# Batch 0's column attention and its reading of x placed among units 2 and 3, the table load placed first, and a new instruction order

## The chip, the cores and the metric

The kernel runs on one core of a Trainium2 chip. The metric is the device time of one execution in microseconds (us), lower being better. TensorE is called PE, VectorE DVE, ScalarE ACT, GpSimd POOL; SP is the engine whose queue issues most of the DMAs.

## The reference

Attention in two directions between x (8 batches, 8 heads, 512 positions, 64 wide) and a state (32 rows per head), and a feed-forward layer over the 4608 joined rows, with a rational function between its two products:

```python
a = softmax(scale * x @ state.T, over the state rows)          # row attention
xread = a @ state
a2 = softmax(scale * state @ x.T, over the 512 positions)      # column attention
sread = a2 @ x
X = concat([xread, sread], axis=2), heads joined to 512 columns # 4608 x 512
h = X @ w_in                                                   # 512 -> 2048
P = a[0] + a[1]*h + a[2]*h*h + a[3]*h*h*h
Q = 1 + |b[0]|*|h| + |b[1]|*h*h
out = (P / (Q + 1e-6)) @ w_out                                 # 2048 -> 512
```

## The kernel before, in words

**Units.** The hidden width of 2048 is cut into 8 slices of 256. Unit n is batch n // 8 with slice n % 8; units 64 to 71 are the 256 sread rows of all batches. A unit's tiles are 128x1024. Its steps, each a token of the order below: `F:n:0` and `F:n:1` (front, L818; 6 matmuls of 512 columns each) make h in PSUM; ACT makes `FC` (C, L830) and `FB` (A, L837); DVE runs `mu` (L841), `po` (L845) and `qd` (L851), which read h in PSUM; ACT `qa`, `ln`, `ex` (L857, L928, L938) make the reciprocal; DVE `g1` (gh, L862), `g2` (L868), `g3` (L874); POOL `gl` (L881). The second product is `mh:n:t` (4 matmuls with gh) and `ml:n:t` (2 matmuls with gl), for four groups t of 128 rows (L891); they add up over 8 units in four PSUM banks o0 to o3. h stays in its PSUM tile until `po`.

**Front of a batch.** xread is never formed: a unit multiplies the row attention aT with m = state times a slice of w_in. `X:i` (L715, 32 small matmuls) makes m for two batches, `XA:i` copies it out of PSUM on ACT (L733), `xs:i` stores it and `lm`, `fs`, `ft` load and split it later (a high and a low part, so that fp32r matmuls keep the precision). For batch 0 `fh` and `fo` (L747 on ACT, L751 on DVE) take it straight from PSUM.

**Weights.** They come in as 64-bit words and are turned into fp32 on the chip, in groups 0 to 15 of 1 MB (slices of w_in and w_out in turns): `lr` loads a half on SP's queue, `cp` (ACT, L300), `jr` (DVE, L313) and `jl` (DVE, L331) convert; for w_out `wh` (ACT, L346) and `wl` (POOL, L353) split it. The tiles `cv_y` and `cv_r` of `cp` and `jr` share four buffers; the result of a w_out group lies in `cv_r` until both `wl` are done. `ws` stores a converted slice, `lw` loads it again for later batches.

**Attention of batch 0.** It is made in halves by its own functions: `scores0:g` (PE, L397 in `scores`), `sc_copy0:g` (ACT, L533), `row_T0:g` (PE, L547), `row_max0`, `row_sub0`, `row_sum0` (DVE, L568 to L587), `row_exp0` (ACT), `row_norm0` (POOL, L592), `a_T0`, `a_hi0`, `a_lo0` (L596 to L614), which make aT for units 0 to 7. Its column attention is `col_max:0` (L414), `col_scale:0` (L418), `col_exp:0:j` (ACT, L444), `col_eps:0`, `col_norm:0` (L472, L476), the transposes `e2_T0:j` (L616, into o2 and o3) and copies `e2_copy0:j` (L621), then `sread:0:g` (PE, L638, reads x), `sr_copy:0` (L650), `sr_T:0`, `sr_fin:0` (L661). Nothing but units 64 to 71 needs its result. Batches 1 to 7 use `e2_T` and `e2_copy` (L481, L486) with one tile of two banks.

**PSUM.** Beside o0 to o3 there are two tiles of two banks each, tag "h" (`ps_h`), shared by h, the X tiles, scores, `e2_T` and sread.

**Order.** `ORDER` is a list of tokens, found by a search and written out by hand; the loop at the end calls one function for each token, and each engine issues its instructions in that order. So a token that waits holds back all later ones on its own engine, and no others. Cross-engine waits and the choice of a free buffer are made when the program is built. `pre` loads the activation table set; `lc`, `cb`, `cv`, `b0a` bring in the constants; `ls:a:b` loads the state of batches a to b - 1 (on ACT's queue if a is 0, else SP's); `lx` loads the next piece of x or of x transposed, in the order in which they are used.

Of the kernel before, what the change touches and what calls it, by code (L numbers as in the profile page):

```python
# [199 lines left out]
def attention_rational_ffn(  # L200
# [159 lines left out]
    def load_win(n):  # L360
# [3 lines left out]
        win_t[n] = t  # L364

    TS, AT, X = {}, {}, {}
    xseq, x_at = [], [0]  # L370

    def load_next_x():
        i = x_at[0]
        if i == len(xseq):
            return
        x_at[0] += 1
# [689 lines left out]
```

## Time and profile before

| what | value |
|---|---|
| median of 3 runs | 663.66 us (663.57 to 663.66) |
| profiled execution | 663.7 us, its span 661.9 us |
| PE busy | 642.4 us, 97% of the span |
| DVE busy | 622.2 us, 94% |
| ACT busy | 520.3 us, 79% |
| POOL busy | 310.1 us, 47% |
| DMA moved | 85.67 MB |
| mean granted clock of PE | 0.996 of full |

Busy time is the time in which an engine has an instruction running; matmuls overlap, so a busy PE need not be at its peak. The span runs from the first instruction's start to the last one's end. A row of the time line gives the start, the length, the engine, the line of the kernel, and in brackets how long the engine sat idle before and what ended that.

### The profile page before, as it was taken

The page shows a single profiled execution, that of the slowest core. Times are in us where ns is not written, and L with a number is a line of the kernel's source. Part 1 is how long each engine was busy: PE and PEld are TensorE (multiplying, and loading weights), DVE is VectorE, ACT ScalarE, POOL GpSimd, SP SyncE. Part 2 cuts the span into 40 slices and gives each one's busy share as a digit, 9 for nine tenths or more (in the row PEclk, how much of TensorE's full clock was granted, in tenths as well). Part 3 has the DMA queues.
Part 4 walks back from the last instruction along what each step waited for, and adds up shares of the span by engine and source line. Part 5 has one row for each costly group of instructions (what it writes and reads, how often), then busy time and mean ns, then how long its engine had stood idle before and what let it go on. Part 6 is the DMA issues. An engine that isn't in the chain of part 4 may idle for free.

```text
span 661.9 us, 11289 instructions
## 1 busy us (share of the span) xinstructions
PE 642.4 (97%) x4474; PEld 509.8 (77%) x4474; DVE 622.2 (94%) x585; ACT 520.3 (79%) x634; POOL 310.1 (47%) x174
## 2 busy tenths in 40 slices
PE   5689999999999999999999999999999999999997
PEld 2556677877878877878878888878788888888995
DVE  5999999899998997999999999999999999899886
ACT  5989999887968688877777887859787768784772
POOL 1254346535454434545443564445554454455550
PEclk9999999999999999999999999999999999999999
DMA  9969987144417162314213220204322010101411
GB/s 346 407 213 394 328 303 254 34 143 138 143 45 245 52 239 97 128 48 144 82 50 125 100 93 17 80 32 144 109 83 81 32 65 32 49 33 51 142 49 32
DMA packets 30679, 85.67 MB, mean 129 GB/s; under 512 B 3490, under 2 KB 3618, under 8 KB 30626
## 3 DMA queue, kind: packets, MB, share of 16 engines
q1 hardware_dynamic: 30290, 84.56, 36.4%
q8 instruction: 35, 0.57, 0.4%
q10 hardware_dynamic: 336, 0.39, 0.3%
q14 instruction: 18, 0.15, 0.1%
HBM read 57.15 MB, written 27.79 MB: 128 GB/s over the span
## 4 chain that ended last, share of the span: by engine, by line
PE 91%; ACT 4%; DVE 2%; issue 1%; POOL 1%; DMA 1%; ACTq 0%; POOLq 0%
PE h L818 29%; PE ps_x L715 3%; PE o__1521 L891 2%; PE o__2974 L891 2%; PE o__5848 L891 2%; PE o__1530 L891 2%; PE o__2242 L891 2%; PE o__4128 L891 2%; PE o__4759 L891 2%; PE o__2979 L891 2%; PE o__4143 L891 2%; PE o__2215 L891 2%; PE o__2250 L891 2%; PE o__2199 L891 2%; PE o__4167 L891 2%; PE o__3564 L891 2%
## 5 line engine op out<-in xcount | busy, mean ns | idle before, releaser
L881 POOL TENSOR_TENSOR gl<-C,L 128x1024 fp32r<-128x1024 f32 (+1 forms) x70 | 171.4, 2451 | 226.3 <-DVE C L874 155.2
L818 PE MATMUL h<-aT,m 128*128 128x512 f32 x768 | 186.9, 391 | 0.2 <-ACT xo_w L733 0.2
L818 PEld LDWEIGHTS h<-aT,m 128*128 128x128 f32 x768 | 143.4, 188 | 32.6 <-ACT xo_w L733 1.0
L830 ACT ACTIVATE C<-h,cst 128x1024 f32<-128x1024 f32 (+1 forms) x72 | 83.3, 1157 | 38.9 <-PE h L818 26.5
L764 POOL TENSOR_TENSOR m<-m_sb,m 128x512 fp32r<-128x512 f32 x56 | 81.7, 1463 | 59.8 <-ACT m L760 56.1
L862 DVE SCALAR_TENSOR_TENSOR gh<-C,cst,L 128x1024 fp32r<-128x1024 f32 (+1 forms) x72 | 93.3, 1297 | 9.9 <-ACT L L938 8.2
L837 ACT ACTIVATE A<-h,cst 128x1024 f32<-128x1024 f32 (+1 forms) x72 | 76.8, 1066 | 30.1 <-PE h L818 24.0
L851 DVE SCALAR_TENSOR_TENSOR A<-A,b0a,h 128x1024 f32<-128x1024 f32 (+1 forms) x72 | 87.2, 1213 | 4.7 <-ACT A L837 3.6
L874 DVE SCALAR_TENSOR_TENSOR C<-C,cst,A 128x1024 f32<-128x1024 f32 (+1 forms) x72 | 89.4, 1244 | 1.5
L845 DVE SCALAR_TENSOR_TENSOR C<-C,cst,h 128x1024 f32<-128x1024 f32 (+1 forms) x72 | 87.5, 1218 | 1.7
L857 ACT ACTIVATE A<-A 128x1024 f32<-128x1024 f32 (+1 forms) x72 | 72.8, 1011 | 19.8 <-DVE A L851 19.8
L868 DVE SCALAR_TENSOR_TENSOR A<-A,gh 128x1024 f32<-128x1024 f32 (+1 forms) x72 | 86.5, 1201 | 1.8
L841 DVE TENSOR_TENSOR C<-C,h 128x1024 f32<-128x1024 f32 (+1 forms) x72 | 82.9, 1152 | 1.8 <-ACT C L830 1.8
L928 ACT ACTIVATE L<-A 128x1024 f32<-128x1024 f32 (+1 forms) x72 | 73.0, 1013 | 3.0
L938 ACT ACTIVATE L<-L 128x1024 f32<-128x1024 f32 (+1 forms) x72 | 72.7, 1013 | 1.7
L715 PE MATMUL ps_x<-win_sb,st 64*32 64x256 f32 x1024 | 35.8, 393 | 3.3 <-ACT xo_w L733 1.8
L760 ACT CAST m<-m_sb 128x512 fp32r<-128x512 f32 x56 | 34.2, 613 | 4.0 <-PE h L818 3.7
L353 POOL TENSOR_TENSOR wo<-cv_r,wo 128x512 fp32r<-128x512 f32 x16 | 24.7, 1564 | 22.1 <-ACT wo L346 22.1
L715 PEld LDWEIGHTS ps_x<-win_sb,st 64*32 64x32 f32 x1024 | 17.4, 109 | 18.7 <-issue 5.9
L818 PEld LDWEIGHTS h<-sh,m 128*128 128x128 f32 x192 | 23.9, 191 | 0.6
L818 PE MATMUL h<-sh,m 128*128 128x256 f32 x192 | 24.1, 283 | 0.0
L733 ACT COPY xo<-ps_x 128x1024 f32<-128x1024 f32 (+1 forms) x24 | 20.7, 872 | 1.5 <-PE ps_x L715 1.3
(245 smaller groups left out, 1106.6 us busy)
## 6 DMA issues: line engine op xcount, KB each, us to landing
m_sb<-m_dram SPq DMA_DIRECT2D x56, 256.0 KB, 3.1
xT_sb<-in_xT_dram SPq DMA_DIRECT2D x16, 512.0 KB, 5.5
x_sb<-in_x_dram SPq DMA_DIRECT2D x16, 512.0 KB, 5.7
m_dram<-xo SPq DMA_DIRECT2D x16, 512.0 KB, 3.7
win_sb<-w_in_dram SPq DMA_DIRECT2D x16, 512.0 KB, 4.3
out_dram<-o_sb SPq DMA_DIRECT2D x32, 256.0 KB, 3.5
raw<-in_w_in_dram SPq DMA_DIRECT2D x10, 512.0 KB, 8.1
raw_w<-in_w_out_dram SPq DMA_DIRECT2D x8, 512.0 KB, 8.8
```

The source lines that it names most:

```text
L764: nc.gpsimd.tensor_tensor(m[:, 1], MF.pop(n), m[:, 0].bitcast(F32), op=ALU.subtract)
L818: nc.tensor.matmul(h[:, ci * W : (ci + 1) * W], l, r, start=(q == 0), stop=(q == len(seq) - 1),)
L830: nc.scalar.activation(e["C"], e["h"], AF.Identity, scale=cst[:, 3:4], bias=cst[:, 2:3])
L837: nc.scalar.activation(e["A"], e["h"], AF.Abs, scale=cst[:, 5:6])
L841: nc.vector.tensor_tensor(e["C"], e["C"], e["h"], op=ALU.mult)
L845: nc.vector.scalar_tensor_tensor(e["C"], e["C"], cst[:, 1:2], e["h"], op0=ALU.add, op1=ALU.mult)
L851: nc.vector.scalar_tensor_tensor(e["A"], e["A"], b0a, e["h"], op0=ALU.add, op1=ALU.mult)
L862: nc.vector.scalar_tensor_tensor(e["gh"], e["C"], cst[:, 0:1], e["L"], op0=ALU.add, op1=ALU.mult)
L868: nc.vector.scalar_tensor_tensor(e["A"], e["A"], 1.0 + 1e-6, e["gh"].bitcast(F32), op0=ALU.add, op1=ALU.mult)
L874: nc.vector.scalar_tensor_tensor(e["C"], e["C"], cst[:, 0:1], e["A"], op0=ALU.add, op1=ALU.subtract)
L881: eng.tensor_tensor(e["gl"], e["C"], e["L"], op=ALU.mult)
L891: nc.tensor.matmul(O[t], e[l][:, j * W + x : j * W + x + P], WO[u][:, j, k, :], start=(u == 0 and l == "gh" and k == 0 and j == 0), stop=( ...
```

## The change

The order list is new throughout. Up to unit 3 it differs as shown; behind that it is again a list of the same tokens with other neighbours. Batch 0's column attention, which stood ahead of units 0 and 1 and between them, now stands among units 1 to 3 (`col_max:0` ahead of `g1:1`, `sread:0` behind `g1:2`), and uses `e2_T` and `e2_copy` with a two-bank tile, as the other batches do; `e2_T0` and `e2_copy0` are gone. `pre` stands ahead of the first copy on ACT. The first state load brings one batch instead of two. Loads of x and of x transposed are tokens of their own with batch and half (`lx:b:g`, `lt:b:g`); from batch 4 on the transposed x uses the buffers of the X copies (tag "xo").

```diff
--- before.py
+++ after.py
 ORDER = [
-    "ls:0:2 lx scores0:0 sc_copy0:0 lr:0:0 cp:0:0 jr:0:0 jl:0:0 row_T0:0 pre lc cb row_max0:0 "
-    "row_sub0:0 lx cv b0a scores0:1 sc_copy0:1 lr:0:1 jr:0:1 cp:0:1 col_max:0 jl:0:1 row_T0:1 "
-    "col_scale:0 row_exp0:0 row_max0:1 row_sub0:1 row_sum0:0 ls:2:8 col_exp:0:0 col_exp:0:1 lr:1:0 "
-    "cp:1:0 X:1 row_norm0:0 lr:1:1 row_exp0:1 row_sum0:1 XA:1 X:0 jr:1 fh:0 XA:0 row_norm0:1 cp:1:1 "
-    "X:2 XA:2 fo:0 jl:1 a_T0:0 a_hi0:0 a_lo0:0 a_T0:1 X:4 a_hi0:1 a_lo0:1 lr:2:0 cp:2:0 lr:2:1 jr:2 "
-    "F:0:0 F:0:1 cp:2:1 col_eps:0 col_norm:0 XA:4 lr:3:0 jl:2 fh:1 fo:1 F:1:0 lr:4:0 cp:4:0 cp:3:0 "
-    "lr:3:1 cp:3:1 F:1:1 jr:3 jl:3 e2_T0:1 lr:4:1 FB:0 jr:4 FC:0 wh:3 wl:3:1 FB:1 qd:0 lx mu:0 lx "
-    "lr:5:0 lr:5:1 qa:0 ln:0 ex:0 qd:1 e2_T0:0 po:0 wl:3:0 e2_copy0:0 e2_copy0:1 sread:0:0 sread:0:1 "
-    "lr:6:0 lr:6:1 cp:5:0 jr:5 g1:0 mh:0:3 ws:0 xs:1 g2:0 cp:5:1 FC:1 jl:5 sr_copy:0 sr_T:0 qa:1 ln:1 "
-    "xs:0 sr_fin:0 g3:0 mu:1 po:1 mh:0:2 wh:5 lr:7:0 lr:7:1 X:8 X:5 cp:4:1 jl:4 cp:6:0 fh:2 mh:0:1 "
-    "fo:2 ex:1 g1:1 gl:0 ml:0:2 xs:4 lr:8:0 XA:8 cp:6:1 cp:7:0 cp:7:1 ws:1 xs:2 XA:5 lr:8:1 jr:7 "
-    "F:2:0 F:2:1 FC:2 FB:2 wl:5:0 wl:5:1 mh:1:3 g2:1 xs:5 X:6 XA:6 jl:7 wh:7 mh:1:2 g3:1 gl:1 cp:8:0 "
-    "lr:9:0 ws:2 X:12 XA:12 jr:6 wl:7:0 qd:2 mu:2 po:2 mh:0:0 ml:0:0 mh:1:0 fh:3 fo:3 X:9 qa:2 ln:2 "
-    "ex:2 lr:9:1 wl:7:1 jl:6 ml:0:3 xs:6 XA:9 lr:11:0 cp:8:1 lr:11:1 cp:9:0 cp:9:1 g1:2 jr:9 X:10 "
-    "XA:10 F:3:0 F:3:1 FC:3 g2:2 xs:12 mh:2:1 jl:9 jr:8 wh:9 xs:9 lr:10:0 lr:10:1 g3:2 jl:8 xs:8 "
-    "ml:0:1 mh:2:2 FB:3 qd:3 wl:9:0 X:16 mu:3 XA:16 gl:2 fh:4 xs:10 ml:1:0 cp:11:0 ml:1:3 mh:2:0 qa:3 "
...
+    "lt:0:0 ls:0:1 pre scores0:0 sc_copy0:0 lc cb cv b0a lr:0:0 cp:0:0 jr:0:0 jl:0:0 lt:0:1 row_T0:0 "
+    "row_max0:0 scores0:1 sc_copy0:1 row_T0:1 row_sub0:0 lr:0:1 jr:0:1 cp:0:1 row_exp0:0 ls:1:8 "
+    "jl:0:1 X:1 row_max0:1 row_sub0:1 row_exp0:1 X:0 XA:1 lr:1:0 lr:1:1 X:2 row_sum0:0 row_sum0:1 "
+    "row_norm0:0 lr:2:0 cp:1:0 row_norm0:1 a_T0:0 lr:2:1 XA:0 jr:1 a_T0:1 fh:0 fo:0 lr:3:0 cp:1:1 "
+    "XA:2 jl:1 X:4 a_hi0:0 a_lo0:0 a_hi0:1 a_lo0:1 cp:2:0 cp:2:1 jr:2 XA:4 jl:2 fh:1 fo:1 F:0:0 "
+    "cp:3:0 lr:3:1 lr:4:0 lr:4:1 jr:3 cp:3:1 jl:3 cp:4:0 xs:1 jr:4 F:0:1 FC:0 lr:5:0 lr:5:1 FB:0 qd:0 "
+    "wh:3 F:1:0 F:1:1 FB:1 qa:0 ln:0 ex:0 cp:5:0 mu:0 cp:5:1 wl:3:0 qd:1 FC:1 po:0 cp:4:1 lr:7:0 "
+    "wl:3:1 lr:7:1 X:5 XA:5 ws:0 jr:5 g1:0 mh:0:0 xs:0 qa:1 ln:1 X:8 XA:8 jl:5 lx:0:0 wh:5 mh:0:1 "
+    "lr:6:0 lr:6:1 mh:0:2 mh:0:3 g2:0 g3:0 mu:1 xs:5 lx:0:1 po:1 jl:4 fh:2 fo:2 gl:0 cp:6:0 cp:7:0 "
+    "jr:7 wl:5:0 col_max:0 ex:1 g1:1 cp:7:1 xs:4 X:9 XA:9 cp:6:1 ml:0:1 wl:5:1 jl:7 xs:2 F:2:0 F:2:1 "
+    "FB:2 FC:2 lr:8:0 X:6 mh:1:2 lr:9:0 lr:8:1 g2:1 XA:6 mh:1:1 col_scale:0 g3:1 gl:1 ml:0:0 "
+    "col_exp:0:0 qd:2 ws:1 wh:7 col_exp:0:1 mh:1:3 mu:2 X:12 xs:6 col_eps:0 po:2 mh:1:0 XA:12 ml:0:3 "
+    "qa:2 wl:7:0 jr:6 fh:3 fo:3 ml:0:2 col_norm:0 jl:6 e2_T:0 ln:2 ex:2 g1:2 lr:9:1 e2_copy:0 ml:1:3 "
+    "X:10 XA:10 cp:8:0 sread:0:0 sread:0:1 sr_copy:0 jr:8 ml:1:1 g2:2 ws:2 cp:8:1 lr:11:0 F:3:0 "
+    "lr:11:1 cp:9:0 cp:9:1 sr_T:0 sr_fin:0 F:3:1 FB:3 wl:7:1 jr:9 jl:8 mh:2:1 xs:8 FC:3 g3:2 X:16 "
+    "fh:4 mh:2:2 gl:2 jl:9 wh:9 qd:3 fo:4 xs:10 lr:12:0 qa:3 mh:2:0 ml:2:1 XA:16 ln:3 ml:1:0 ex:3 "
+    "mu:3 po:3 X:14 XA:14 wl:9:1 X:13 lr:10:0 lr:10:1 ml:1:2 cp:11:0 cp:11:1 jr:11 g1:3 cp:10:0 xs:9 "
...
 ]
@@ attention_rational_ffn
     TS, AT, X = {}, {}, {}
-    xseq, x_at = [], [0]
-
-    def load_next_x():
-        i = x_at[0]
-        if i == len(xseq):
-            return
-        x_at[0] += 1
-        what, b, g = xseq[i]
-        if what == "xT":
-            t = ld.tile([P, NP, S // 2], F32, name="xT_sb", tag="x")
-            nc.sync.dma_start(t, xT[b, g])
-        else:
-            t = ld.tile([P, NT // 2, DM], F32, name="x_sb", tag="x")
-            nc.sync.dma_start(t, x[b, g])
-        X[xseq[i]] = t
+    def load_xT(b, g):
+        pool, tag = (ld, "x") if b < 4 else (ew, "xo")
+        t = X["xT", b, g] = pool.tile(
+            [P, NP, S // 2], F32, name="xT_sb", tag=tag, bufs=2
+        )
+        nc.sync.dma_start(t, xT[b, g])
+
+    def load_x(b, g):
+        t = X["x", b, g] = ld.tile(
+            [P, NT // 2, DM], F32, name="x_sb", tag="x", bufs=2
+        )
+        nc.sync.dma_start(t, x[b, g])
...
-    def e2_T0(j):
-        T = TS[0]
-        T["pe", j] = obank("ps_e0", 2 + j)
-        transposes0(T["pe", j], T["e2"][:, j])
-
-    def e2_copy0(j):
-        T = TS[0]
-        if j == 0:
-            T["e2T"] = at.tile([P, 2, S], F32, name="e2T", tag="e2T")
-        nc.scalar.copy(T["e2T"][:, j], T["pe", j])
...
-        e2_T0,
-        e2_copy0,
...
-        "lx": load_next_x,
+        "lx": load_x,
+        "lt": load_xT,
...
-    for name, args in tokens:
-        if name in ("scores0", "scores", "sread"):
-            b, g = (0, *args)[-2:]
-            xseq.append(("x" if name == "sread" else "xT", b, g))
```

## Rows read from the trace of the kernel before

**Rows 1.** The page, part 1: busy us (share of the span) and instructions of each engine.

```profile
PE 642.4 (97%) x4474; PEld 509.8 (77%) x4474; DVE 622.2 (94%) x585; ACT 520.3 (79%) x634; POOL 310.1 (47%) x174
```

**Rows 2.** Stretches: busy us of PE, PEld, DVE, ACT, POOL; clock; DMA share, GB/s.

```profile
20.00:30.00 10.00, 6.73 (x37) 5.24 (x32) 9.75 (x13) 9.94 (x14) 2.50 (x2) 1.00 1.03 411
30.00:40.00 10.00, 8.00 (x141) 5.42 (x142) 9.90 (x11) 9.93 (x17) 4.24 (x2) 0.83 0.95 347
40.00:50.00 10.00, 8.82 (x93) 5.88 (x92) 9.96 (x9) 8.38 (x12) 5.84 (x4) 1.00 0.44 143
...
70.00:80.00 10.00, 10.00 (x92) 7.28 (x77) 9.54 (x10) 9.81 (x12) 5.16 (x3) 1.00 1.01 347
640.00:650.00 10.00, 10.00 (x67) 9.05 (x67) 9.02 (x13) 6.68 (x12) 2.94 (x2) 1.00 0.21 76
```

**Rows 3.** The chain that ended last: start us, us, engine, tile, line, count.

```profile
54.40 3.03 PE h L818 x12
...
73.51 0.91 PE o__485 L891 x4
...
92.96 2.72 PE h L818 x12
...
97.49 1.02 PE ps_x L715 x32
...
107.69 0.88 PE ps_e L423 x8
...
111.33 1.03 PE ps_sr L638 x64
```

**Rows 4.** Time line of ACT, up to 32 us.

```profile
7.50 1.28 ACT L949 ACT_TABLE_LOAD   x1
8.79 0.17 ACT L253 COPY cst<-ps_c 128x6 f32<-128x6 f32 x1
...
12.42 0.72 ACT L444 ACTIVATE e<-sT,cm 128x512 f32<-128x512 f32 x1 [0.94 <-DVE cm L418]
...
30.37 1.06 ACT L625 COPY e2T<-ps_e 128x512 f32<-128x512 f32 x2
```

**Rows 5.** Time line of DVE, up to 40 us.

```profile
10.42 1.22 DVE L414 TENSOR_REDUCE cm<-sT 128x2 f32<-128x1024 f32 x1 [0.49 <-ACT sT L533]
...
15.99 0.25 DVE L587 RECIPROCAL rs<-rs 128x16 f32<-128x16 f32 x1
...
28.95 1.27 DVE L845 SCALAR_TENSOR_TENSOR C<-C,cst,h 128x1024 f32<-128x1024 f32 x1
...
39.15 0.68 DVE L751 TENSOR_TENSOR m<-ps_x,m 128x512 fp32r<-128x512 f32 x1
```

**Rows 6.** Time line of PE, 30 to 44 us.

```profile
30.99 0.32 PE L638 MATMUL ps_sr<-x_sb,e2T 128*32 128x64 f32 x8 [4.26 <-ACT e2T L625]
...
38.12 1.10 PE L715 MATMUL ps_x<-win_sb,st 64*32 64x256 f32 x32 [0.67 <-DVE C L845]
...
40.64 2.92 PE L818 MATMUL h<-aT,m 128*128 128x512 f32 x12
```

**Rows 7.** Time lines of POOL, DVE and ACT, 38 to 66 us.

```profile
38.11 4.51 POOL L353 TENSOR_TENSOR wo<-cv_r,wo 128x512 fp32r<-128x512 f32 x2
...
64.06 1.28 POOL L353 TENSOR_TENSOR wo<-cv_r,wo 128x512 fp32r<-128x512 f32 x1
...
41.39 1.78 DVE L313 TENSOR_SCALAR cv_r<-raw_w 128x1024 int32<-128x1024 uint32 x1
...
46.56 0.68 DVE L313 TENSOR_SCALAR cv_r<-raw_w 128x1024 int32<-128x1024 uint32 x1
...
42.65 1.26 ACT L300 ACTIVATE cv_y<-raw_w 128x512 f32<-128x512 f32 x2 [1.62 <-POOL wo L353]
```

**Rows 8.** Time line of DVE: the waits ahead of g1:2 and g1:7.

```profile
53.48 1.28 DVE L862 SCALAR_TENSOR_TENSOR gh<-C,cst,L 128x1024 fp32r<-128x1024 f32 x1 [0.41 <-ACT L L938]
...
116.55 1.28 DVE L862 SCALAR_TENSOR_TENSOR gh<-C,cst,L 128x1024 fp32r<-128x1024 f32 x1 [1.08 <-ACT L L938]
```

310 rows, old and new, of the table ORDER are left out of this document.

## The prediction

> **What bounds the kernel now.** I read four views in this order. The page's engine table says that TensorE (PE) is busy 97% and VectorE (DVE) 94% [rows 1]: neither has much to give on average. The table by stretches shows that they are not full at the same time [rows 2]: from the row 70 to 80 us to the row 640 to 650 us PE is busy all the time (10.00 of 10), while from 20 to 40 us it is at 6.7 and 8.0 of 10 and DVE and ScalarE (ACT) are at 9.8 to 9.9. So what ends last is PE's queue; its matmuls are the same in both kernels, and the time changes by what PE wins or loses before it is full. The chain of waits has the hand-over: up to 54.4 us it runs through ACT, from F:3 at 54.40 on through PE [rows 3]. Fourth, each engine's queue ahead of that point, in order of time [rows 4 to 8]. In the list of waits PE stands for a DMA only once, at the first scores, and never for x.
>
> The profiled execution is 663.7 us, a span of 661.9 and 1.8 around it; the median of three runs is 663.66, so I sum against 663.7 and take nothing off. About 0.2% (1.3 us) is what a measurement of this kernel can tell from no change.
>
> **Part 1, ahead of unit 2.** ACT's queue loses the second table load, 1.28 us at 7.50, and two column exponentials, 0.7 us each from 12.42 (0.94 us of waiting stood before them), and later the two e2 copies (1.06) and the small copies of sread [rows 4]. DVE's queue loses col_max, 1.22 us [rows 5], and three tiny entries. None of this is free, since both run full here. I walk the new list through the queues, with the step from one row's start to the next as the price. The constants now stand ahead of the first conversion (cp:0:0 about 0.5 us later), the second scores are no longer behind them (0.5 earlier), and without col_max row_sum0:1 ends at about 14.6 instead of 16.24 [rows 5]. Some of these 1.6 us go back: XA:0 now stands ahead of fh:0 on ACT, so fo:0 waits on DVE with jl:1 and a_lo0 behind it; FC:0 now precedes FB:0, so qd:0 waits; po:0 ends at 29.1 instead of 30.2 and fo:2 at 38.8 instead of 39.8 [rows 5]: a lead of 1.0.
>
> Of the table load, first the row: 1.28 us, and the next ACT instruction 0.01 us behind it [rows 4]. The Trainium skill (ScalarE: Activation LUTs, What ACT_TABLE_LOAD costs) adds a drain of 1.38 us, so that ACT would win 2.66. The trace has no such gap there; the sum goes by the row.
>
> PE: its wait of 4.26 us for the e2 copy, up to 30.99 [rows 6], isn't won. The sread that stood there goes, but X:5, next in the new list, needs the bank that F:0 holds until po:0, so PE stands from about 24.3 to 29.2. The granted clock was 0.83 over 30 to 40 us [rows 2], a part of it at 1.2 instead of 2.4 GHz, right behind that wait. I take it to be so again, and it costs nothing: behind X:5 the next X waits for a copy that ACT reaches only at about 33.1, and PE catches up under it. Up to F:2 PE does the same work in both lists to 0.1 us (X:9 and four mh matmuls come, 1.02 + 0.91; e2_T0, sread and sr_T go, 0.88 + 1.03 + 0.11) [rows 3]. F:2 stood at 40.64, behind an X that waited for po:1 until 38.12 [rows 6]; now X:9 follows po:1 at 37.1, then ml:0:1, and F:2 starts at fo:2's end, 38.9. **Lead 1.7.**
>
> **Part 2, among units 2 and 3.** The column work comes back. DVE's queue up to g1:2 holds the very same 50 entries in both lists, so only waits can be won or lost in it. One stands out: jr:7 took 1.78 us where jr:6 took 0.68, and it ended 0.55 us behind the second of two weight splits on GpSimd (POOL, 38.11 + 4.51 = 42.62) [rows 7]. The new list puts jr:7 right behind fo:2, again under these two splits, with col_max and g1:1 behind it on DVE; mh:1:2 on PE waits for that g1:1. Bounds: 0 (the splits are over) to 1.10 (the row). I take 0.65, half a split of 1.28 [rows 7], of which 0.4 reaches PE, since X:6 runs before mh:1:2.
>
> The Trainium skill (SBUF — State Buffer, Who interferes with whom) speaks against that place: a DVE instruction with two SBUF inputs or in a two-port mode and a GpSimd one that reads SBUF shut each other out for a whole instruction, in order of issue; a reduction does so never. The rows agree (1.78 against 0.68). By the rule jr:7 could lose a whole split, 1.28, and the sum would be 0.6 us later; col_max loses nothing.
>
> ACT gets col_exp 1.4, e2_copy 1.06 and three small copies between FC:2 and FB:3 [rows 4]. Their cover: it stood 1.62 us at 42.65 [rows 7], was busy only 8.4 of 10 from 40 to 50 us [rows 2], and enters the stretch with the load and the exponentials saved; without that cover they would push ex:2 and XA:10, and F:3 waits for a bank that such an XA frees. PE had 11.35 us of matmuls from F:2 to F:3 (F:2 2.72, four mh at 0.91, two ml at 0.45, four X at 1.02) [rows 3] in the 13.76 us from 40.64 to 54.40, so 2.4 us dead. The new list has 13.6 us there (one X less, e2_T:0, sread and three ml more: 0.88 + 1.03 + 1.36). The two-bank tiles now share the two pairs of banks with X and F: e2_T:0 takes one that is free at po:2 or fo:3, sread waits for its copy behind ex:2. I keep 2.4 us dead, the nearest row, in the same place; ends 0.5 and 4.
>
> **Part 3, the rest.** x later takes 1 MB off a full DMA (share 1.03 from 20 to 30 us) [rows 2], but no engine waited for those weights: 0. On SP's queue the later transposed loads have buffers of their own and weight loads stand ahead of x; PE never waited for them: 0. From unit 8 on the new list changes as often between kinds of matmul as the old: 0 ± 0.3. DVE waited 1.08 us for ACT at g1:7 [rows 8]; that wait is set by PE's own F:7, and up to there DVE's 111 entries are again the same, so a lead of PE carries through. The tail holds the same last instructions, with one ml less behind F:71 as cover: 0 to 0.45, I take 0.
>
> **Sum:** -1.7 (F:2) + 0.4 (jr:7) + 0 = -1.3, and 663.7 - 1.3 = **662.4 us**.
>
> **Rivals.** *More is won.* Column work fills ACT's and PE's gaps, and PE's 2.4 us halve: -1.3 - 1.2 = -2.5, **661.2**. For it: PE has more small matmuls queued there. Against: sread waits for a copy behind ex:2.
>
> *A buffer on ACT: slower.* cp:7:0 waited 1.62 us for the last split of group 5, until 42.62 [rows 7]. The new list puts cp:7:0 ahead of ex:1 and so of g1:1; before, both were past. If buffers are handed out in the same way and that split ends at 41.3, ACT stands from 38.1 to 41.3. From cp:7:0 to ex:2 ACT took 10.8 us (42.65 to 53.45; g1:2 waited for it until 53.48 [rows 8]); the new list adds ex:1, XA:9, cp:6:1 and col_exp and takes out XA:5 and cp:8:0, by the spacing of such rows 2.4 more. 41.3 + 13.2 = 54.5, so ex:2 comes 1.0 later than before, and F:3 and g1:2 with it: **664.7**, with a second such wait 665.2. The point from which it decides is a split that ends after 40.3. For it: the same buffers, the same wait. Against: which buffer is free is not in the trace, and jl:4 frees two others at about 38.2.
>
> *The change does nothing.* DVE's queue is the same up to g1:2 and g1:7; if its dead time to there is merely moved, PE is held at unit 7 as before: **663.7** ± 0.6.
>
> **How the numbers follow.** Forecast (-0.6 to -2.0): 0.38, half of it beyond -1.3. More won: 0.24. Nothing: 0.14. Buffer: 0.24. Faster by over 0.2%: 0.19 + 0.24 + 0.01 = 0.44; within: 0.19 + 0.13 + 0.01 = 0.33; slower: 0.23. The forecast's own range is 661.7 to 663.1; to hold 8 in 10 the range reaches into both neighbours and to the ends of the dead time, 660.4 to 665.2.
>
> **What would show it.** Right: no table load at 7.5; po:0 ends near 29; F:2 starts near 39 and F:3 between 54 and 55; PE full from there on. cp:7:0 waiting on POOL for over 2 us shows the buffer, a jr:7 of over 1.3 us the collision. I am wrong if PE waits again after 60 us, or if F:8 starts later than the old list's although F:2 was early.

## The result, and the profile after

The changed kernel takes **672.02 us** (median of 4 runs, 671.74 to 673.69) against 663.64 us of the kernel before (663.57 to 663.66): a ratio of 1.0131, 95% interval 1.0119 to 1.0143. It is slower by 8.4 us, outside the range of the prediction. The profiled span is 670.0 us. Line numbers of the changed kernel are 15 lower from the front on (L803 for L818, L876 for L891); in the experiments they shift a little with each edit.

The page, part 1, and part 4 by engine, of the kernel after:

```profile
PE 650.7 (97%) x4474; PEld 511.2 (76%) x4474; DVE 629.2 (94%) x585; ACT 521.3 (78%) x632; POOL 307.4 (46%) x174
...
PE 79%; ACT 7%; DVE 6%; issue 3%; DMA 3%; POOL 1%; SPq 0%; ACTq 0%; DVEq 0%; POOLq 0%
```

The same row of part 4 for the kernel before:

```profile
PE 91%; ACT 4%; DVE 2%; issue 1%; POOL 1%; DMA 1%; ACTq 0%; POOLq 0%
```

The 4474 matmuls of [rows 1] are busy 8.3 us longer, and the chain that ended last has left PE for 21% of the span instead of 9%. So there are two questions: why the same matmuls take longer, and where PE waits.

Stretches of the kernel after, columns as in [rows 2]:

```profile
20.00:30.00 10.00, 5.61 (x37) 3.90 (x44) 9.87 (x11) 9.94 (x13) 2.50 (x2) 0.96 0.96 339
30.00:40.00 10.00, 9.90 (x111) 5.96 (x96) 9.93 (x10) 9.45 (x13) 5.42 (x3) 0.87 0.93 342
40.00:50.00 10.00, 9.74 (x98) 6.54 (x97) 10.00 (x12) 9.88 (x15) 5.10 (x4) 1.00 0.88 314
...
70.00:80.00 10.00, 9.79 (x76) 7.02 (x68) 9.58 (x10) 9.75 (x14) 5.76 (x3) 1.00 0.98 350
...
160.00:180.00 20.00, 18.93 (x84) 14.92 (x83) 19.66 (x17) 12.40 (x16) 7.60 (x5) 1.00 0.46 145
180.00:200.00 20.00, 19.08 (x158) 14.68 (x164) 19.75 (x19) 15.47 (x20) 9.58 (x5) 1.00 0.12 40
```

The last two stretches in the kernel before:

```profile
160.00:180.00 20.00, 20.00 (x121) 16.18 (x106) 19.66 (x20) 18.62 (x23) 10.01 (x7) 1.00 0.42 135
180.00:200.00 20.00, 20.00 (x204) 15.70 (x202) 18.74 (x18) 13.81 (x19) 10.36 (x5) 1.00 0.25 89
```

From 30 to 50 us PE is fuller than before (9.90 and 9.74 where [rows 2] has 8.00 and 8.82). But it isn't full from there on: 9.79 from 70 to 80 us, and 38.0 of 40 from 160 to 200 us, where it was full before.

The head (everything up to unit 2) came out as forecast. Time lines of DVE, PE and ACT, after:

```profile
27.78 1.27 DVE L830 SCALAR_TENSOR_TENSOR C<-C,cst,h 128x1024 f32<-128x1024 f32 x1
...
38.00 0.68 DVE L736 TENSOR_TENSOR m<-ps_x,m 128x512 fp32r<-128x512 f32 x1
38.60 1.17 DVE L314 TENSOR_SCALAR cv_r<-raw_w 128x1024 int32<-128x1024 uint32 x1
...
29.20 1.96 PE L700 MATMUL ps_x<-win_sb,st 64*32 64x256 f32 x32 [4.39 <-DVE C L830]
...
38.74 3.02 PE L803 MATMUL h<-aT,m 128*128 128x512 f32 x12
...
53.99 1.55 PE L803 MATMUL h<-aT,m 128*128 128x512 f32 x6
...
1.19 1.28 ACT L934 ACT_TABLE_LOAD   x1 [1.19 <-PEq L1030]
...
38.12 0.68 ACT L301 ACTIVATE cv_y<-raw_w 128x512 f32<-128x512 f32 x1 [0.52 <-DVE win_sb L332]
```

po:0 ends at 29.05, fo:2 at 38.68, F:2 starts at 38.74 (forecast 29.1, 38.8, 38.9). jr:7 takes 1.17 us, between 0.68 and 1.78 [rows 7]. cp:7:0 (the row at 38.12) waits 0.52 us for jl:4, which frees its buffers, as the prediction's argument against that rival had it, and never for POOL; so the rival of the buffer falls. F:2 leads by 1.9 us, F:4 by 1.3 and F:8 by 0.5 (113.89 against 114.35).

To place the loss I took from the traces the distance of each matmul's end from the last one's, less the usual distance for its shape (0.2266 us for 512 columns, and so on), and added this up by stretches: what PE loses, by waits or by slower matmuls, us:

```
run                  0-60  60-120 120-160 160-200 200-300 300-end    sum
before              18.20    2.72    0.63    0.69    1.52    3.45  27.20
after               15.98    4.74    1.21    3.66    2.69    7.43  35.71
e2_before_wo_moved  18.42    3.13    1.05    1.04    2.60    7.75  33.99
e1_after_wo_back    16.05    4.77    0.74    4.83    1.80    3.27  31.46
e3_head             15.87    4.99    0.90    0.60    1.59    3.41  27.36
e8_head_fs8         15.91    4.45    0.66    0.69    1.40    3.49  26.60
e7_middle           16.45    4.56    0.90    0.55    3.16    3.14  28.76
e9_two_steps        17.03    4.30    0.76    2.20    1.77    3.18  29.24
e12_all_mended      15.94    4.07    0.75    2.16    1.72    3.18  27.82
e13_three_meetings  16.00    4.11    0.76    2.08    1.71    3.17  27.84
e14_dve_full        16.45    4.10    0.76    0.39    1.72    3.24  26.67
```

(The profiled execution of e1 took 667.51 us, 1.4 over its median, so its row overstates its loss: PE waited twice, 1.0 and 0.9 us, up to 180.9 us, and its granted clock was 0.66 of full from 180 to 185 us, where the kernel after has 1.00 in spite of two such waits.) In the kernel after, the first 60 us win 2.2 us; 2.0 of them go by 120 us, 3.0 more are lost from 160 to 200 us, and from 200 us to the end 5.2 drain away a little at a time. The last of these is hardly waiting: PE is busy all the time there, and the matmuls of the second product are some 4 ns slower on average, as the first group of experiments shows.

### The profile page after: what moved, and what is told of

It is laid out like the page before. It is cut to its first block, busy times and chain, and to the rows that moved or that the text cites. A ratio compares the mean times of both kernels' runs of the same rounds, so it can differ in the third digit from the quotient of the medians.

```text
span 670.0 us, 11266 instructions
## 1 busy us (share of the span) xinstructions
PE 650.7 (97%) x4474; PEld 511.2 (76%) x4474; DVE 629.2 (94%) x585; ACT 521.3 (78%) x632; POOL 307.4 (46%) x174
## 4 chain that ended last, share of the span: by engine, by line
PE 79%; ACT 7%; DVE 6%; issue 3%; DMA 3%; POOL 1%; SPq 0%; ACTq 0%; DVEq 0%; POOLq 0%
PE h L803 25%; PE ps_x L700 2%; PE o__2277 L876 2%; PE o__2236 L876 2%; PE o__2951 L876 2%; PE o__2940 L876 2%; PE o__4772 L876 2%; PE o__3591 L876 2%; PE o__4123 L876 2%; PE o__2969 L876 2%; PE o__5331 L876 2%; PE o__5856 L876 2%; PE o__3572 L876 2%; PE o__4128 L876 2%; PE o__3577 L876 2%
## 5 line engine op out<-in xcount | busy, mean ns | idle before, releaser
L803 PE MATMUL h<-aT,m 128*128 128x512 f32 x768 | 188.1, 392 | 0.6 <-DVE m L736 0.6
L803 PEld LDWEIGHTS h<-aT,m 128*128 128x128 f32 x768 | 143.2, 188 | 35.0 <-DVE m L736 2.3
L822 ACT ACTIVATE A<-h,cst 128x1024 f32<-128x1024 f32 (+1 forms) x72 | 76.6, 1068 | 38.8 <-PE h L803 34.6
L749 POOL TENSOR_TENSOR m<-m_sb,m 128x512 fp32r<-128x512 f32 x56 | 78.0, 1400 | 56.7 <-ACT m L745 56.0
L859 DVE SCALAR_TENSOR_TENSOR C<-C,cst,A 128x1024 f32<-128x1024 f32 (+1 forms) x72 | 91.0, 1265 | 1.6
L700 PEld LDWEIGHTS ps_x<-win_sb,st 64*32 64x32 f32 x1024 | 19.3, 113 | 19.4 <-issue 10.2
L803 PEld LDWEIGHTS h<-sh,m 128*128 128x128 f32 x192 | 24.1, 191 | 0.7
L803 PE MATMUL h<-sh,m 128*128 128x256 f32 x192 | 24.3, 283 | 0.0
L504 POOL TENSOR_TENSOR e<-e,rs 128x512 f32<-128x512 f32 x14 | 17.7, 1276 | 13.2 <-DVE rs L498 9.8
```

The lines of the kernel that those rows point to most:

```text
L749: nc.gpsimd.tensor_tensor(m[:, 1], MF.pop(n), m[:, 0].bitcast(F32), op=ALU.subtract)
L803: nc.tensor.matmul(h[:, ci * W : (ci + 1) * W], l, r, start=(q == 0), stop=(q == len(seq) - 1),)
L822: nc.scalar.activation(e["A"], e["h"], AF.Abs, scale=cst[:, 5:6])
L859: nc.vector.scalar_tensor_tensor(e["C"], e["C"], cst[:, 0:1], e["A"], op0=ALU.add, op1=ALU.subtract)
```

## The experiments

**The place of wo.** A pool gives each tile its place in the order in which the tiles are first asked for. The small tiles cm and r2 of the column attention (two buffers of 32 bytes each, 128 in all) were asked for ahead of the eight wo tiles; with `col_max:0` moved behind unit 1 they are asked for after six of them. Those six start 128 bytes lower in each partition; other large tiles trade places among themselves, but keep their starts modulo 256 bytes. (These places follow from the order of requests and the sizes in the kernels' text.) wo is what the second product streams; the tile whose columns it loads is gh or gl.

Run e1, the changed kernel:

```diff
     srT = cp.tile([P, NP, B * NS], F32, name="srT")
+    for tag in ("cm", "r2"):
+        cp.tile([P, 2], F32, name=tag, tag=tag, bufs=2)
```

> The changed kernel, order list untouched; only the four 32-byte slots of cm and r2 are asked for ahead of the wo tiles, as they were in the kernel before, so that all eight wo tiles start at the addresses of before (96 bytes past a multiple of 256) and not six of them 128 bytes lower. Theory A (the place of wo costs the time): the 1132 back-to-back second-matrix matmuls on the six tiles come some 4 to 5 ns sooner each, 4 to 6 us in all: 666 to 668 us. Theory B (the new list itself loses, by waits sown through the run): the address does nothing, 672.0 us within 0.6.

Measured: 666.07 us (5 runs), ratio 1.0045 (1.0032 to 1.0059) to before. 5.95 of the 8.4 us are gone with no instruction moved.

Run e2, the kernel before:

```diff
     srT = cp.tile([P, NP, B * NS], F32, name="srT")
+    for tag in ("w5", "w7", "w6", "w4", "w0", "w1"):
+        cp.tile([P, 4 * CW, 2], U32, name="rsv", tag=tag)
+    for tag in ("cm", "r2"):
+        cp.tile([P, 2], F32, name=tag, tag=tag, bufs=2)
```

> The kernel before, order list untouched; only the wo slots are asked for ahead of those of cm and r2, so that the wo tiles lie where the changed kernel has them, six of eight 128 bytes lower. Theory A: some 1200 matmuls take 4 to 5 ns longer, 5 to 6 us on the path: 668.5 to 670 us. Theory B: 663.6 us within 0.5.

Measured: 670.14 us, ratio 1.0100 (1.0086 to 1.0114), just above the expected range of theory A. The old list pays 6.6 us for the new places. In the table its loss grows in every stretch, and most from 200 us on (5.4 us, against 5.2 in the kernel after).

Is it the address of wo, or its distance from something? Run e5, the kernel before:

```diff
+    cp.tile([P, 32], F32, name="pad", tag="pad")
     ident = cp.tile([P, P], F32, name="ident")
```

> The kernel before, order list untouched; 128 unused bytes ahead of every tile, so that all of them, wo and gh and gl and the rest, start 128 bytes higher and all at 224 past a multiple of 256. Theory A1 (it is the place of wo by itself that counts): all eight wo tiles are now at the slow residue, 669 to 672 us. Theory A2 (it is the distance between wo, which the second-matrix matmul streams, and the tile whose columns it loads, gh or gl): that distance is a multiple of 256 again, 663.5 us within 0.5.

Measured: 663.57 us, ratio 1.0000 (0.9991 to 1.0009). The slow address is as fast as the old one if everything moves with it: the distance counts. Run e6 did the same with all tiles at multiples of 512 bytes (a pad of 160 bytes, `ones` in the slot of a wo):

> The kernel before, order list untouched; all large tiles of every pool start at multiples of 512 bytes (before: 352 past one), the tile of ones lying in the slot of a wo. Theory A1: the slots are at a residue not tried yet; the odd map's 3.2 to 6.1 ns at every residue say 667 to 671 us, unless a multiple of 512 is better than any. Theory A2: 663.5 us within 0.5. A gain (under 662.8) would say that a start at a multiple of 64 is worth something by itself.

Measured: 663.76 us, ratio 1.0002 (0.9993 to 1.0011). None of the three starts tried (96, 224 and 0 past a multiple of 256) is better by itself. Run e10 leaves wo alone and moves gh and gl, in the kernel before:

```diff
     def first(n):
+        if n == 0:
+            ew.tile([P, 32], F32, name="pad", tag="pad", bufs=1)
         e = EW[n]
```

> The kernel before, order list untouched; 128 unused bytes ahead of the four slots of gh and gl alone, wo and all the rest at their addresses of before. Theory A2 (the distance between wo and the tile whose columns the second-matrix matmul loads): all 1632 of these matmuls are slow, some 5 ns each, 8 us in all: 670 to 672 us. Rival (the distance between wo and some other tile, C, A, L, m or win, that another engine reads or writes at the time): 663.6 us within 0.5.

Measured: 672.39 us, ratio 1.0130 (1.0116 to 1.0144), just above the expected range. e2 moved wo against everything else, e10 moved gh and gl against everything else; the one pair that both moved is wo with gh and gl. VectorE and GpSimd write gh and gl, so they could be the ones in wo's way; but in e10's trace a matmul came every 232.3 ns while one of them was writing and every 232.5 ns while neither was. So it is the distance between the two operands of one matmul stream. Two more runs put the eight wo tiles at eight different starts each, with reserved slots and unused tiles of 32 or 64 bytes between them:

> The kernel before with its order; the eight wo tiles stand at eight different residues, 64 bytes apart (224, 288, 352, 416, 480, 32, 96 and 160 past a multiple of 512), everything else but the state's two tiles where it was. Theory A with a period of 256 bytes: matmuls that stream wo from 224 and 480 take 4 to 5 ns longer than those from 96 and 352, the others tell what lies between; with a period of 512 only 224 is slow. Theory B: all eight alike, within 1 ns, and 663.6 us.

> As the odd map, all eight wo tiles 32 bytes higher: 256, 320, 384, 448, 0, 64, 128 and 192 past a multiple of 512, that is 96 and 32 bytes below and 32 and 96 bytes above the residue of gh. Theory A2: every one is at a distance that is no multiple of 256, so all are slow, 3 to 6 ns a matmul, about 670 us. Rival (only distances of 64 and more count): the tiles at 32 bytes' distance as fast as at none, about 667 us.

Measured: 670.01 and 673.09 us (one run each). The mean distance from one matmul's end to the next, over the back-to-back ones of the second product, by the distance of wo from gh or gl modulo 256 bytes:

```
run                  distance: matmuls, ns
before               0: 1504, 227.6
after                0: 378, 228.9    128: 1133, 232.6
e1_after_wo_back     0: 1501, 227.5
e2_before_wo_moved   0: 376, 228.9    128: 1132, 232.6
e5_all_128           0: 1505, 227.7
e10_gh_alone       128: 1509, 232.4
e4_map_odd           0: 381, 229.9     64: 374, 230.9    128: 368, 232.0    192: 384, 232.7
e11_map_even        32: 381, 232.5     96: 374, 233.5    160: 370, 233.4    224: 385, 233.2
```

At distance 0 a matmul costs 227.6 ns, elsewhere 231 to 233.5; a tile at distance 0 among others at other distances pays some of it too (229 to 230; why, no run shows). The period is 256 and not 512: of e4's two tiles at distance 0, one lies at 0 modulo 512 and one at 256, and they took 230.1 and 229.8 ns. In e11 32 bytes cost as much as the rest, so its rival falls. The 1511 pairs of the kernel after at 231.7 on average make 1511 x 4.1 ns = 6.2 us. The view of the tile wo has it as well: the duration of the matmuls into one output tile, for the tile with its last rows near 412 us (minimum, median, maximum ns), in before, after, e5 and e10:

```profile
L891 PE MATMUL o__3585<-wo,gh x32: 389/389/393, 353.5 to 407.7; 128*128 128x512 f32 x32
```

```profile
L876 PE MATMUL o__3572<-wo,gh x32: 387/393/399, 357.6 to 410.2; 128*128 128x512 f32 x32
```

```profile
L892 PE MATMUL o__3586<-wo,gh x32: 389/389/393, 353.2 to 407.4; 128*128 128x512 f32 x32
```

```profile
L893 PE MATMUL o__3586<-wo,gh x32: 391/393/405, 357.2 to 412.4; 128*128 128x512 f32 x32
```

A median of 389 where the distance is 0, 393 where it is 128: one per cent on a row, with no wait in it.

**The head alone.** Runs e3 and e8 take the new order up to the gh step of unit 7 and the old list from there, wo at its old place.

> Everything up to the gh step of unit 7 in the changed kernel's order (batch 0's column attention among units 1 to 3, the table load first, x loaded later), from there on the list of the kernel before; wo at the addresses of before. Theory A: the head gains what the prediction said, and nothing else is in the way: 662.4 us, 661.9 to 663.0. Theory B (the head's lead is given back by unit 8, as the trace of the changed kernel hints, where F:8 leads by 0.46 us against 1.4 at F:6): 663.2 us, 662.9 to 663.7. If the head itself is what loses: over 664.5 us.

Measured: 663.51 us (11 runs), ratio 0.9997 (0.9989 to 1.0006): the head by itself is no loss, and its lead is given back. Where, the time lines of SP's queue, ACT and DVE of e3 tell:

```profile
89.07 1.38 SPq L751 DMA_DIRECT2D m_sb<-m_dram  x1
...
94.92 0.62 ACT L754 CAST m<-m_sb 128x512 fp32r<-128x512 f32 x1 [2.12 <-DMA m_sb<-m_dram]
95.45 1.11 ACT L831 ACTIVATE A<-h,cst 128x1024 f32<-128x1024 f32 x1
96.46 1.19 ACT L824 ACTIVATE C<-h,cst 128x1024 f32<-128x1024 f32 x1
...
97.69 1.28 DVE L845 SCALAR_TENSOR_TENSOR A<-A,b0a,h 128x1024 f32<-128x1024 f32 x1 [0.86 <-ACT C L824]
```

The new list has `lm:8 fs:8` next to each other: ACT stands 2.12 us for the load, with A and C of unit 6 behind it in its queue, and DVE stands 0.86 us for C. Run e8 moves that one token:

```diff
-... row_sub:1 lm:8 fs:8 g3:5 F:6:0 ... col_exp:1:0 ml:5:2 xs:29 fh:7 ...
+... row_sub:1 lm:8 g3:5 F:6:0 ... col_exp:1:0 ml:5:2 xs:29 fs:8 fh:7 ...
```

> As the run of the head alone, with one step moved: the copy of the high part of unit 8's m (fs:8, ScalarE) stands ahead of that of unit 7 (fh:7) and no longer right behind its own load, where ScalarE waits 2.12 us for the transfer and hands C of unit 6 to VectorE 0.86 us late. Theory H (the head's lead of 1.3 us is spent on this wait): 0.86 us come back, 662.7 us, 662.3 to 663.0. Rival (VectorE, which meets the same steps of batch 1's attention either way, sets unit 8): 663.5 us, as the head alone.

Measured: 662.83 us (11 runs), ratio 0.9994 (0.9985 to 1.0003). The median is 0.68 us under e3's, near the expected 0.86, but the interval reaches over 1, so it isn't shown by this run alone. The traces of the full list show it better. F:12 in before, after and e12 (the new list with fs:8 moved, below):

```profile
133.90 2.43 PE L818 MATMUL h<-aT,m 128*128 128x512 f32 x10
```

```profile
133.78 2.44 PE L803 MATMUL h<-aT,m 128*128 128x512 f32 x10
```

```profile
132.55 3.79 PE L812 MATMUL h<-aT,m 128*128 128x512 f32 x16
```

At F:6 the kernel after leads by 1.4 us and e12 by 1.7; at F:12 the one has 0.1 of it left, the other 1.35. That is more than the 0.86 us of the wait; how much of it is another difference between the two executions, these traces don't tell.

One thing that the head's size hangs on is not in any list: the granted clock behind PE's long wait. Stretches 30 to 40 us of e9 and e12, which have the same instructions up to there:

```profile
30.00:40.00 10.00, 10.00 (x115) 5.54 (x100) 9.93 (x9) 9.50 (x14) 5.12 (x3) 0.73 0.95 337
```

```profile
30.00:40.00 10.00, 9.91 (x107) 5.91 (x90) 9.93 (x10) 9.44 (x14) 5.71 (x3) 0.88 0.92 334
```

F:2 leads by 0.7 us in e9 and by 2.2 in e12. Over the nine traces with this head, F:2 comes 17.0 us behind F:1 in the three with a clock of 0.87 to 0.89 there (after, e8, e12), and 17.4 to 17.9 us behind it in the six with 0.73 to 0.81 (e1, e3, e7, e9, e13, e14). So up to 0.9 us between two of these traces can be this, and a comparison of single traces, e3 with e8 or e9 with e12, holds it too.

**The middle of the list.** What the list loses by itself (666.07 against 663.54) stands in one stretch of the table, 160 to 200 us. Run e7 takes the old order for units 8 to 20 alone:

> The changed kernel's order but for the stretch from the gh step of unit 7 to that of unit 20, which follows the list of the kernel before; wo at the addresses of before. Theory M (what the new list loses by itself, 666.1 against 663.5, is lost in units 8 to 20, where three of VectorE's entries meet GpSimd's and take 1 to 1.4 us longer each): 663.5 us, 663.0 to 664.3. Rival (it is lost in small waits all along): 665.2 us or more.

Measured: 664.44 us, ratio 1.0015 (1.0006 to 1.0024), just above the expected range. 1.6 of 2.5 us come back; the table has 0.55 for it from 160 to 200 us, but 3.16 from 200 to 300, where the others at this place of wo have 1.4 to 1.8, behind the seam to the new list. So the middle seems to be most of it; the seam leaves open how much.

Time lines of POOL and DVE in that stretch, run e1:

```profile
158.73 2.39 DVE L868 SCALAR_TENSOR_TENSOR C<-C,cst,A 128x1024 f32<-128x1024 f32 x1
158.74 1.29 POOL L758 TENSOR_TENSOR m<-m_sb,m 128x512 fp32r<-128x512 f32 x1
...
162.50 2.41 POOL L875 TENSOR_TENSOR gl<-C,L 128x1024 fp32r<-128x1024 f32 x1 [2.46 <-PE o__1500 L885]
163.36 2.63 DVE L470 TENSOR_TENSOR e<-e,mx 128x1024 f32<-128x1024 f32 x1
...
169.41 1.59 POOL L758 TENSOR_TENSOR m<-m_sb,m 128x512 fp32r<-128x512 f32 x1 [4.50 <-ACT m L754]
169.89 2.19 DVE L862 SCALAR_TENSOR_TENSOR A<-A,gh 128x1024 f32<-128x1024 f32 x1
```

Three DVE entries with two operands in SBUF began with or under a POOL instruction and took 2.39, 2.63 and 2.19 us; by the usual 1.28, 1.22 and 1.23 that is 3.5 us too long. Each ends 1.1 us behind POOL's end, a little less than its own length. DVE waits for nothing from 150 to 182 us, so what is lost on it stays lost, and PE, which had no wait from 150 to 205 us in the kernel before, waits three times there (1.0, 0.9 and 0.3 us). Run e9 moves two of the three out of POOL's way:

```diff
-... tr1:2 fs:14 os:7:1 ft:14 lm:17 ml:10:3 g3:12 XA:11 mh:12:3 row_max:2 FC:13 ... gl:12 row_sub:2 row_exp:2 ...
+... tr1:2 fs:14 os:7:1 ft:14 lm:17 ml:10:3 row_max:2 row_sub:2 g3:12 XA:11 mh:12:3 FC:13 ... gl:12 row_exp:2 ...
```

> The changed kernel with wo at the addresses of before, and two entries of VectorE moved: row_max and row_sub of batch 2 stand ahead of g3 of unit 12, so that the subtraction (two operands in SBUF) no longer begins while GpSimd forms gl of unit 12, and g3 no longer as GpSimd splits m of unit 14. Theory C (what the new list loses by itself is lost where VectorE and GpSimd meet in units 12 to 13: 2.39, 2.63 and 2.19 us in place of 1.21 to 1.28): some 2.4 of 3.4 us come back on VectorE, and TensorE, which waits for it there, has most of it: 663.6 to 664.5 us. Rival (the order on GpSimd, where gl of unit 13 stands behind the normalization of batch 2 and TensorE waits 0.9 us for it, or batch 2's attention as such): 665.5 us or more.

Measured: 664.76 us (11 runs), ratio 1.0015 (1.0006 to 1.0024): 1.3 us come back, just short of what was expected. PE's loss from 160 to 200 us is 2.2 us, where the kernel after has 3.7. With fs:8 moved as well:

> The changed kernel with the three repairs together: wo at the addresses of before, the two entries of VectorE moved, and fs:8 ahead of fh:7. If the three are what the change costs, and the head's 1.3 us are then kept: 662.5 us, 662.0 to 663.2. Rival (each is taken up by the next wait): 663.5 us or more.

Measured: 664.37 us, ratio 1.0011 (1.0003 to 1.0020). The rival holds: PE was 0.9 us ahead at 120 us (20.0 lost against 20.9), and 160 to 200 us still cost 2.16. Its trace showed the third meeting (g3 of unit 13, 2.38 us) and PE waiting 0.92 us for gl of unit 13. Run e13 moves both:

```diff
-... gl:12 row_exp:2 ... ml:12:2 fs:16 ft:16 mu:13 ... FB:14 lx:2:0 ... row_norm:2:1 col_exp:2:0 ... e2_T:2 gl:13 ml:13:0 ...
+... gl:12 row_exp:2 ... ml:12:2 mu:13 ... FB:14 fs:16 ft:16 lx:2:0 ... gl:13 row_norm:2:1 col_exp:2:0 ... e2_T:2 ml:13:0 ...
```

> As the run with all mended, and two more entries moved: ScalarE copies the high part of unit 16's m behind A of unit 14 and not ahead of it, so that GpSimd's split of it no longer begins in the same moment as g3 of unit 13 (2.38 us for 1.28); and GpSimd forms gl of unit 13 ahead of the normalization of batch 2, not behind it (TensorE waited 0.92 us for it). Theory C (the list's own loss is meetings of VectorE and GpSimd and the wait behind them in units 12 to 14): 1.5 us more come back, 662.8 us, 662.2 to 663.4, and with that the 1.3 us of the head show. Rival (a further wait takes them up): 664.0 us or more.

Measured: 664.14 us, ratio 1.0012 (1.0003 to 1.0021): the rival again. Time lines of DVE and PE of e13:

```profile
166.28 1.28 DVE L856 SCALAR_TENSOR_TENSOR gh<-C,cst,L 128x1024 fp32r<-128x1024 f32 x1 [0.93 <-ACT L L932]
...
172.56 1.15 DVE L506 TENSOR_SCALAR rs<-rs 128x32 f32<-128x32 f32 x1
...
180.07 1.19 PE L885 MATMUL o__1513<-wo,gh 128*128 128x512 f32 x4 [0.96 <-DVE gh L856]
```

The meetings of the three entries are gone, and two other costs are left: qd of unit 13, behind row_sub since e9, makes its exp late on ACT (0.93 us, in e9 and e12 too), and the moved gl held row_eps (1.15 us for 0.18). PE waits for g1 of unit 14, the end of that queue. Run e14 takes these two away as well:

```diff
-... ml:10:3 row_max:2 row_sub:2 g3:12 XA:11 mh:12:3 FC:13 FB:13 qd:13 qa:13 ...
+... ml:10:3 row_max:2 FB:13 qd:13 row_sub:2 g3:12 XA:11 mh:12:3 FC:13 qa:13 ...
-... gl:13 row_norm:2:1 ... e2_T:2 ml:13:0 ml:13:2 ... ml:11:0 mh:14:3 ...
+... row_norm:2:1 ... e2_T:2 gl:13 ml:11:0 ml:13:0 ml:13:2 ... mh:14:3 ...
```

> As the run with all mended (two entries of VectorE and fs:8 moved, wo at the addresses of before), the stretch of batch 2's attention mended without a new wait: A and qd of unit 13 come ahead of row_sub and g3 of unit 12 (so that exp of unit 13 is ready in time; VectorE waited 0.93 us for it), the split of unit 16's m comes behind A of unit 14 as in the last run, gl of unit 13 keeps its place behind the normalization (ahead of it, it met row_eps: 1.15 us for 0.17), and TensorE has one ml more ahead of its wait for it. Theory D (VectorE is full from 150 to 181 us in either list, and every us that it loses there is TensorE's): about 1.5 of its 1.9 us come back, 663.0 us, 662.4 to 663.6. Rival: 664 us or more.

Measured: **662.84 us** (11 runs, 662.17 to 663.89), ratio 0.9989 (0.9980 to 0.9998) to the kernel before. The time line of DVE of e14:

```profile
160.84 1.22 DVE L470 TENSOR_TENSOR e<-e,mx 128x1024 f32<-128x1024 f32 x1
161.98 1.28 DVE L868 SCALAR_TENSOR_TENSOR C<-C,cst,A 128x1024 f32<-128x1024 f32 x1
...
167.16 1.23 DVE L862 SCALAR_TENSOR_TENSOR A<-A,gh 128x1024 f32<-128x1024 f32 x1
```

All three entries are back at their own length, and 160 to 200 us cost 0.39 us, less than before. With wo at its distance and eight tokens in other places, the change is faster than the kernel before too, by 0.8 us, in an interval that just clears 1.

## Why the prediction was wrong

- **"Its matmuls are the same in both kernels, and the time changes by what PE wins or loses before it is full."** This step failed first, and for the most: 5.95 of the 8.4 us (e1), 6.6 by the counter-proof (e2). The instructions were the same; their operands lay elsewhere. I took the length of a matmul from a row of before without asking what sets it, and read `col_max:0` as an entry on DVE alone. It is also the first request for two tiles, and the change moved that request behind the requests for wo.
- **"From unit 8 on ... 0 ± 0.3."** The second failure, 2.5 us. I compared how often the lists change between kinds of matmul, which stayed near nothing, and didn't ask when DVE's and POOL's entries fall together in a part whose list is new throughout. I weighed that meeting at one instruction, jr:7, where it cost 0.5 us; the stretch around batch 2's attention had three of it, 3.5 us on DVE. e9 and e14 took them away, and the waits behind them, and 160 to 200 us went from 3.66 us of loss (in the kernel after, a little of it wo's) to 0.39.
- **"... so a lead of PE carries through."** By the rows wrong at one token at least: fs:8 right behind its load (2.12 us on ACT, 0.86 on DVE). With it moved, 1.35 us of lead are left at F:12 instead of 0.1; by the times alone (e3 to e8, e9 to e12) its price of 0.4 to 0.7 us is not shown. That DVE's entries up to g1:7 are the same is true; the prediction drew from it that only DVE's own order matters, but ACT's order around them had changed.
- **The head was right** up to F:2, in place and size: F:2 at 38.74 against 38.9, PE standing until 29.20 against 29.2, the clock of 30 to 40 us at 0.87 (0.83 taken), jr:7 held by 0.5 us (0.65 taken), the table load at 1.19 us ahead of all data. The size was in part luck: the prediction said of the low clock that "it costs nothing", and in the traces with a clock of 0.73 to 0.81 F:2 comes 0.4 to 0.9 us later. What of the head reaches the end is less than the 1.3 us forecast: nothing in e3, 0.8 us in e8, not clear of noise. That the likeliest time, 662.4, is near e14's 662.84 is no proof of the sum either; e14 had to move eight tokens for it.
- **Of the rivals** none was the cause. "A buffer on ACT" had the right sign and the wrong mechanism: cp:7:0 never waited for POOL. "The change does nothing" gave the time of the head alone (663.7 against e3's 663.51), but by dead time on DVE's queue, where e3's rows show ACT waiting for a load. Of the signs of being wrong one came: PE waits again after 60 us. The larger loss, that of the second product, comes without any sign that the prediction named.

The sum of the parts: 5.95 (place) + 1.3 (two meetings, e1 to e9) + 0.4 (fs:8, e9 to e12) + 1.5 (the third meeting and what stood behind it, e12 to e14) = 9.2, which is 672.02 - 662.84. Each of the small steps alone is near what a run can tell, so only the 5.95 and the sum of the rest (3.2) are shown; the order in which they were taken sets how they share.

## What to carry to other kernels

When an order changes, look not only at the queues but at which tile is asked for first, because places in SBUF follow from it; compare one row's median per matmul in both profiles before looking for waits. If every stretch loses a little and nothing is waiting, suspect the price of an instruction; here moving a few bytes told it in one run. In a stretch where VectorE has no gap, an entry with two SBUF operands shouldn't begin under a GpSimd instruction, and a lead of TensorE that VectorE or ScalarE can't follow is given back.

## What the runs showed of the hardware

The streamed and the loaded operand of a matmul are not independent of each other in SBUF: with their starts a multiple of 256 bytes apart a 512-column matmul came every 227.6 ns, at other distances every 231 to 233.5 ns (e4, e10, e11); the absolute start made no difference at the three places tried (e5, e6). What in the memory does this, and whether other tile sizes show the same period, no run here tells. The Trainium skill (SBUF — State Buffer, Who interferes with whom) gives TensorE two independent read ports, one for the moving operand and one for the weights, and says it waits for no one; by these runs the two still cost each other about 2%.

VectorE's entries with two SBUF operands took 2.19 to 2.63 us in place of 1.22 to 1.28 where they began with or under a GpSimd instruction (e1), while reductions beside one kept 1.21 and 1.22 (e13, e9). The Trainium skill (SBUF — State Buffer, Who interferes with whom) says that a VectorE instruction with two SBUF inputs contends with a GpSimd one that reads SBUF, and that the ports they share are locked by one of the two. These rows agree, with each entry ending 1.1 us behind GpSimd's end.
